# Band attention and two MLPs on one core: loads tied to places in TensorE's instruction stream, one mask kind loaded, a last block in halves

## The chip, the cores and the metric

The kernel runs on one core of one Trainium2 chip. The metric is the device time of one execution in microseconds (us), as the median of several executions. A profiled execution gives the trace from which the rows below are taken; its span runs from its first to its last instruction.

## What is computed

Attention over four batches of eight heads: 512 local rows that see keys within 32 positions and the 32 global keys, and 32 global rows that see everything. Its output passes through two MLPs of 2176 rows (4 x 544), width 512 and inner width 2048. All inputs and outputs are 32-bit.

```python
def _attn_ref(q_l, k_l, v_l, q_g, k_g, v_g):
    ...
    s_g = scale * np.matmul(q_g, k_all.transpose(0, 1, 3, 2))
    out_g = np.matmul(sm(s_g), v_all)
    ...
    mask = np.abs(pos[:, None] - pos[None, :]) <= window
    s_ll = np.where(mask, s_ll, -1000000000.0)
    s_l = np.concatenate([s_lg, s_ll], axis=-1)
    out_l = np.matmul(sm(s_l), np.concatenate([v_g, v_l], axis=2))
    ...

# first MLP:  h = x @ w_in; g = elu(h); x = g @ w_out
# second MLP: h = x @ w_in; g = 0 below -1, h above 1, (h + 1)**2 / 4 between; out = g @ w_out
```

## The kernel before

**Stages.** The first 124 us or so are attention, with a first part of the first MLP woven in; then come the two MLPs, in ten chunks of rows of weights, with TensorE nearly without a gap. Each MLP product is made of three matmuls on high and low parts (`wl x xh`, `wh x xl`, `wh x xh`).

**Units of attention.** There are 24 units, n = 0 to 23, in groups of three: the local rows of a pair of heads, the global rows of two pairs, the local rows of the second pair. There are 16 pairs, p = 0 to 15. One turn of the loop issues the scores of unit n (matmuls `s` or `sg`), the transposes of unit n-1 (`pt` or `tg`), the transposes of the output of unit n-2 (`ot`), and the product with the values of unit n-1 (`po` or `pog`). From n = 9 on, 12 matmuls of the MLP (`up`) join in each turn or two. Recording is by a wrapper, `Pinned`, so all of these have one line, L113, and stand in each engine's queue in the order of the program.

**Loads.** All of them are issued by SP (the SyncE queue, SPq), in the order of the program. For each pair these are queries (`q_sb`, 272 KB), keys (`k_sb`, 288 KB) and two halves of the values (`v_sb`, 520 KB each); six pieces of weights (`wraw`, 512 KB) come with them. After the turn of unit n, `arrive(n)` issues the queries and keys of a pair (`load_qk`), a piece of weights or some halves of values; the table `V_UNTIL` tells how far the values may run. `q_sb` and `k_sb` have two buffers each, the values six halves. A paced load (values and weights) also waits until the loads in flight together with it are at most 3200 words of each partition (`IN_FLIGHT`); queries and keys are not paced. So a load's start is set by buffers, pace and SP's order, and not by where TensorE stands.

**Start.** Ten warm-up matmuls on zeros run while queries and keys of pairs 0 and 1, the mask (three kinds, 192 KB, on ACT's queue), the identity and the values of pair 0 are loaded. VectorE copies 32 rows of each of two kinds of the mask.

**End.** `down` sums the last product in four PSUM banks (d = 0 to 3) over two rows of weights; `collect` adds each bank to `acc` on VectorE and stores 128 x 512 results from SP. After attention the order is made by a scheduler (`eng = free`).

## Time and profile before

| what | value |
|---|---|
| median of 3 runs | 863.31 us (861.24 to 863.80) |
| profiled execution | 864.74 us, its span 862.9 us |
| TensorE (PE) busy | 844.9 us, 98% of the span |
| VectorE (DVE) busy | 581.4 us, 67% |
| ScalarE (ACT) busy | 431.7 us, 50% |
| moved by DMA | 65.45 MB, of which code (q8 instruction) 48 packets, 0.79 MB |
| granted TensorE clock, mean | 0.996 of full speed |

A timeline row gives the start, the duration, the engine, the line, the operation, out<-in, the shapes and the count; in brackets stands the idle time of the engine before it and what ended it, where "issue" means that the engine waited for nothing that the profile shows. A row of a stretch gives its length, then busy time and count of each engine, the granted TensorE clock, the busy share of the DMA engines and GB/s. Every TensorE matmul here has a weight load of its own (LDWEIGHTS), a second instruction.

### The profile page before, as it was taken

The numbers are of one execution on the slowest core, as the hardware profiler recorded it, in microseconds if no ns is written. First come the engines' busy times: TensorE is split into PE (matmuls) and PEld (weight loads), VectorE is DVE, ScalarE is ACT, GpSimd is POOL, SyncE is SP. The second block draws the span as 40 slices with busy tenths as digits, with TensorE's granted clock in tenths as the row PEclk, the third lists the DMA queues.
The fourth block names the chain that finished last, engine by engine and source line by source line (L and its number), as shares of the span: only waits on it lengthen the run. The fifth ranks groups of instructions, "written<-read, shape, count | busy, mean of one in ns | idle before, by whom it ended". The sixth has DMA issues, their size and how long they took to land.

```text
span 862.9 us, 14906 instructions
## 1 busy us (share of the span) xinstructions
PE 844.9 (98%) x6138; PEld 694.0 (80%) x6138; DVE 581.4 (67%) x1130; ACT 431.7 (50%) x755; POOL 28.2 (3%) x66
## 2 busy tenths in 40 slices
PE   8799899999999999999999999999999999999998
PEld 5677778888888888888888888888888888888886
DVE  4689765879527964834399896368759754845455
ACT  5678674666335543533357564456435333433332
POOL 2122200000000000000000000000000000000000
PEclk9999999999999999999999999999999999999999
DMA  8888722222101210200022112012101200000014
GB/s 265 288 275 266 222 78 98 97 98 98 50 0 49 98 49 0 98 1 1 0 71 77 49 50 97 1 40 93 63 1 58 90 0 1 1 1 0 2 62 146
DMA packets 23124, 65.45 MB, mean 76 GB/s; under 512 B 3984, under 2 KB 4240, under 8 KB 19344
## 3 DMA queue, kind: packets, MB, share of 16 engines
q1 hardware_dynamic: 22768, 64.23, 21.8%
q8 instruction: 48, 0.79, 0.4%
q10 hardware_dynamic: 288, 0.26, 0.1%
q14 instruction: 20, 0.16, 0.1%
HBM read 60.03 MB, written 4.46 MB: 75 GB/s over the span
## 4 chain that ended last, share of the span: by engine, by line
PE 93%; DMA 3%; DVE 2%; issue 1%; ACT 1%; SPq 0%
PE dn L320 40%; PE up L247 39%; PE up L244 3%; PE dn L337 3%; PE up L113 2%; PE po L113 2%; DMA k_sb<-in_kT 1%; PE pt L113 1%; PE s L113 1%; PE sg L113 1%; PE tg L113 1%; DMA wraw<-in_w 1%; DVE top L113 1%; DMA v_sb<-in_vwin 1%; PE ot L113 1%
## 5 line engine op out<-in xcount | busy, mean ns | idle before, releaser
L320 PE MATMUL dn<-gh,wh 128*128 128x512 f32 x506 | 196.9, 389 | 0.0
L320 PE MATMUL dn<-gl,wh 128*128 128x512 f32 x506 | 196.8, 389 | 0.0
L320 PE MATMUL dn<-gh,wl 128*128 128x512 f32 x506 | 196.3, 390 | 0.0
L247 PE MATMUL up<-xh,wl 128*128 128x512 f32 x492 | 192.5, 391 | 0.0
L247 PE MATMUL up<-xl,wh 128*128 128x512 f32 x492 | 191.6, 389 | 0.0
L247 PE MATMUL up<-xh,wh 128*128 128x512 f32 x492 | 191.6, 389 | 0.0
L278 ACT ACTIVATE gh<-g 128x512 fp32r<-128x512 f32 x123 | 77.7, 632 | 118.7 <-DVE g L267 71.8
L297 DVE TENSOR_TENSOR acc<-dn,acc 128x512 f32<-128x512 f32 x128 | 84.9, 685 | 48.7 <-PE dn L320 48.4
L320 PEld LDWEIGHTS dn<-gl,wh 128*128 128x128 f32 x506 | 95.0, 188 | 19.9
L282 DVE TENSOR_TENSOR gl<-g,gh 128x512 fp32r<-128x512 f32 x123 | 84.6, 689 | 38.9 <-ACT gh L278 37.8
L320 PEld LDWEIGHTS dn<-gh,wh 128*128 128x128 f32 x506 | 95.0, 188 | 19.4
L320 PEld LDWEIGHTS dn<-gh,wl 128*128 128x128 f32 x506 | 95.0, 188 | 19.4
L247 PEld LDWEIGHTS up<-xh,wh 128*128 128x128 f32 x492 | 92.3, 188 | 19.3
L247 PEld LDWEIGHTS up<-xl,wh 128*128 128x128 f32 x492 | 92.4, 188 | 18.8
L247 PEld LDWEIGHTS up<-xh,wl 128*128 128x128 f32 x492 | 92.4, 188 | 18.7
L258 ACT ACTIVATE g<-up,half_sb 128x512 f32<-128x512 f32 (+1 forms) x69 | 47.0, 681 | 113.6 <-PE up L247 104.8
L266 DVE SCALAR_TENSOR_TENSOR g<-g 128x512 f32<-128x512 f32 (+1 forms) x69 | 46.9, 680 | 59.4 <-ACT g L258 59.3
L264 DVE SCALAR_TENSOR_TENSOR g<-up,g 128x512 f32<-128x512 f32 x64 | 43.4, 679 | 62.5 <-ACT g L255 62.5
L253 ACT ACTIVATE g<-up 128x512 f32<-128x512 f32 x64 | 37.8, 590 | 86.2 <-PE up L247 80.6
L267 DVE TENSOR_TENSOR g<-g,e 128x512 f32<-128x512 f32 (+1 forms) x69 | 46.9, 680 | 3.6
L180 ACT ACTIVATE top<-wraw 128x1024 f32<-128x1024 f32 x29 | 33.7, 1163 | 29.2 <-DMA wraw<-in_w 24.1
L255 ACT ACTIVATE g<-g,one_sb 128x512 f32<-128x512 f32 x64 | 45.8, 716 | 1.8
(112 smaller groups left out, 923.6 us busy)
## 6 DMA issues: line engine op xcount, KB each, us to landing
wraw<-in_w SPq DMA_DIRECT2D x29, 1024.0 KB, 4.8
v_sb<-in_vwin SPq DMA_DIRECT2D x32, 520.0 KB, 5.3
k_sb<-in_kT SPq DMA_DIRECT2D x16, 288.0 KB, 3.9
q_sb<-in_qT SPq DMA_DIRECT2D x16, 272.0 KB, 5.2
outT<-acc SPq DMA_DIRECT2D x16, 256.0 KB, 2.1
wraw<-in_w SPq DMA_DIRECT2D x6, 512.0 KB, 4.6
outT<-acc_rows SPq DMA_DIRECT2D x4, 64.0 KB, 2.2
mask_sb<-in_mask ACTq DMA_DIRECT2D x1, 192.0 KB, 3.4
```

The lines of the kernel that those rows point to most:

```text
L113: return lambda *args, **kw: tc.keep_in_program_order(fn(*args, **kw))
L247: eng.tensor.matmul(self.ps, w, x, start=k == 0, stop=k == 3 * KT - 1)
L253: eng.scalar.activation(self.g, self.ps, AF.Exp)
L255: eng.scalar.activation(self.g, self.g, AF.Relu, bias=one_sb, scale=-1.0)
L258: eng.scalar.activation(self.g, self.ps, AF.Relu, bias=half_sb, scale=0.5)
L264: eng.vector.scalar_tensor_tensor(g, self.ps, 0.0, g, ALU.max, ALU.subtract)
L266: eng.vector.scalar_tensor_tensor(g, g, 1.0, g, ALU.min, ALU.mult)
L267: eng.vector.tensor_tensor(g, g, self.e, ALU.add)
L278: eng.scalar.activation(self.gh, self.g, AF.Copy)
L282: eng.vector.tensor_tensor(self.gl, self.g, self.gh.bitcast(F32), ALU.subtract)
L297: eng.vector.tensor_tensor(a, ps, a, ALU.add)
L320: eng.tensor.matmul(banks[d], w[:, d * P:(d + 1) * P], g, start=f == fs[0] and k == 0, stop=f == fs[-1] and k == 2,)
```

## The change

- `Pinned` counts the instructions that it issues to TensorE: 4 for each row of the program that is a 32-bit matmul (it becomes two matmuls, each with its weight load), 2 for the others. When the count passes 186, 436.5, 687 and so on by 250.5, the matmul that passes it is called an entry into a block, and `by_blocks` issues up to three loads behind it: each waits until this matmul is done. The three are chosen by the unit that needs them first: queries and keys of a pair, a half of values, a piece of weights. There are 20 such entries with loads; all loads from pair 2's queries and pair 1's values on go there, and the pace of 3200 words no longer applies to them.
- Queries and keys have three buffers; the third one for keys lies in `acc[0]`, which is written only after attention.
- The mask: only kind 1 (64 KB) is loaded; kinds 0 and 2 are copied whole on VectorE and 32 x 32 of each is filled.
- The last output block (layer 1, last batch, d = 3) is made in two halves of 256 columns, the second of them in a bank of the up products; the first half is stored from ACT's queue, the second from SP's.

```diff
-V_UNTIL = {0: 2, 1: 4, 2: 6, 3: 7, 4: 9, 5: 11}
+AT_ONCE = 3
+
+FIRST_BLOCK, BLOCK = 186, 250.5
...
+            def issue(*args, **kw):
+                ins = tc.keep_in_program_order(fn(*args, **kw))
+                if name in ("matmul", "transpose"):
+                    self.issued += 4 if name == "matmul" and args[1].dtype == F32 else 2
+                    if self.issued > FIRST_BLOCK + self.block * BLOCK:
+                        self.block += 1
+                        at_block(ins)
+                return ins
...
-    def load(out, src, words, paced=True):
+    def load(out, src, words, paced=True, behind=None):
 
         ins = eng.sync.dma_start(out, src)
+        if behind is not None:
+            tc.add_manual_dep(ins.ins, behind.ins.name, LANDED, reason="loads by blocks")
...
+            queue = eng.scalar if at.stop < SL else eng.sync
+            queue.dma_start(outT[d, :, j * S + SG + at.start:j * S + SG + at.stop], a)
...
+            spans = [slice(0, SL)]
+            if (layer, j, fs[-1], d) == (1, B - 1, NF - 1, KT - 1):
+                spans = [slice(0, SL // 2), slice(SL // 2, SL)]
...
+                banks[d] += [up_bank() for _ in spans[1:]]
...
+        qs = [raw_p.tile([P, S], F32, name=f"q_sb{i}") for i in range(3)]
+        ks = [raw_p.tile([P, k_cols], F32, name=f"k_sb{i}") for i in range(2)]
+        ks.append(acc[0].rearrange("p d n -> p (d n)")[:, 0:k_cols])
...
-        eng.scalar.dma_start(mask_sb, mask)
+        load_qk(0)
+        eng.scalar.dma_start(mask_sb[:, 1, :], mask[:, 1, :])
+        load_qk(1)
...
-        eng.vector.tensor_copy(mask_sb[32:64, 0, :], mask_sb[32:64, 1, :])
-        eng.vector.tensor_copy(mask_sb[64:96, 2, :], mask_sb[64:96, 1, :])
+        for kind, r, c in ((0, 0, 0), (2, 96, 64)):
+            eng.vector.tensor_copy(mask_sb[:, kind, :], mask_sb[:, 1, :])
+            eng.vector.memset(mask_sb[r:r + 32, kind, c:c + 32], FILL)
...
+        def by_blocks(ins):
+
+            for _ in range(AT_ONCE):
+                found = []
+                p = now["qk"]
+                if p < len(pairs) and now["n"] >= 3 * ((p - 3) // 2) + 1 + (p - 3) % 2:
+                    found.append((3 * (p // 2) + p % 2 - 1, 0, send_qk))
+                p = len(pairs) - (len(ahead) + 1) // 2
+                if ahead and 2 * len(pairs) - len(ahead) < now["until"]:
+                    found.append((3 * (p // 2) + p % 2 + 1, 1, send_v))
+                if now["free"] and len(parts) < len(halves):
+                    found.append((3 * len(parts) + 3, 2, send_words))
+                if found:
+                    min(found, key=lambda item: item[:2])[2](ins)
...
-            if r == 1 and p + 1 < len(pairs):
-                load_qk(*pairs[p + 1])
-            elif r == 2 and p + 2 < len(pairs):
-                load_qk(*pairs[p + 2])
-            elif r == 0 and g:
-                next(next(sent, iter([0])))
-            while ahead and len(ahead) > 2 * len(pairs) - V_UNTIL.get(n, 4 * g + (4, 6, 7)[r]):
-                load_v(*ahead.pop(0))
+            now["n"] = n
+            if place == 0:
+                return
+            now["until"] = 4 * g + (6, 6, 8)[r]
+            while now["qk"] < len(pairs) and now["qk"] <= p + (r == 2):
+                send_qk()
```

On SP's queue, at the fifth piece of weights (turns n = 14 to 16), there stands before, with the semaphores that each load waits for (DMAHW: an earlier load; PE, DVE, Activation, Pool: that engine):

```order
L113 DMA q_sb<-in_qT 128x544 [waits PE_49,Pool_49]
L113 DMA k_sb<-in_kT 128x576 [waits DMAHW3_49,Pool_49]
L113 DMA v_sb<-in_vwin 128x2x520 [waits DMAHW0_49,PE_49]
L113 DMA wraw<-in_w 128x512 [waits DMAHW1_49,DVE_49,Activation_49]
L113 DMA v_sb<-in_vwin 128x2x520 [waits DMAHW6_49,DMAHW3_49,PE_49]
L113 DMA q_sb<-in_qT 128x544 [waits DMAHW7_49,PE_49,Pool_49]
L113 DMA k_sb<-in_kT 128x576 [waits PE_49]
L113 DMA v_sb<-in_vwin 128x2x520 [waits DMAHW5_49]
L113 DMA v_sb<-in_vwin 128x2x520 [waits DMAHW6_49,DMAHW2_49]
```

and now, from the entry that issues the fifth piece of weights on (`q_sb_126` and so on are the single buffers):

```order
L126 DMA wraw<-in_w 128x512 [waits DMAHW1_49,DVE_49,DMAHW4_49,PE_49,Activation_49]
L126 DMA q_sb_125<-in_qT 128x544 [waits DMAHW5_49,Pool_49]
L126 DMA k_sb_128<-in_kT 128x576 [waits DMAHW6_49,Pool_49]
L126 DMA v_sb<-in_vwin 128x2x520 [waits DMAHW7_49]
L126 DMA v_sb<-in_vwin 128x2x520 [waits DMAHW0_49,PE_49]
L126 DMA q_sb_126<-in_qT 128x544 [waits PE_49,Pool_49]
L126 DMA k_sb_129<-in_kT 128x576 [waits DMAHW2_49]
L126 DMA v_sb<-in_vwin 128x2x520 [waits DMAHW3_49]
L126 DMA v_sb<-in_vwin 128x2x520 [waits DMAHW4_49,PE_49]
```

Here four loads form a block with one wait for TensorE ahead of it, then one half of values stands alone, then four again; before, a load's wait for TensorE was that for its own buffer.

At the end of the program TensorE's last rows were

```order
L320 MATMUL dn<-gl,wh_2887 128x512
L320 MATMUL dn<-gh,wl_2888 128x512
L320 MATMUL dn<-gh,wh_2887 128x512
L320 MATMUL dn<-gl,wh_2887 128x512
L320 MATMUL dn<-gh,wl_2888 128x512
L320 MATMUL dn<-gh,wh_2887 128x512
L320 MATMUL dn<-gl,wh_2887 128x512
```

and are now

```order
L349 MATMUL dn<-gh,wh_2862 128x512
L349 MATMUL dn<-gh,wl_2863 128x256
L349 MATMUL dn<-gh,wh_2862 128x256
L349 MATMUL dn<-gl,wh_2862 128x256
L349 MATMUL dn<-gl,wh_2862 128x512
L349 MATMUL dn<-gh,wl_2863 128x256
L349 MATMUL dn<-gh,wh_2862 128x256
L349 MATMUL dn<-gl,wh_2862 128x256
```

The second half stands some 25 rows earlier (`up<-gh,wl` 128x256 and five more), so that three matmuls of 256 columns end the program, with d = 2 right ahead of them. Between the attention and this end TensorE's, VectorE's and ACT's orders are as before, but for the name of the third key buffer.

## Rows read from the trace of the kernel before

**Rows 1.** Waits of TensorE, first 130 us: us in total, times, longest

```profile
PE s L113 <- issue: 2.8, 3, 1.8
PE pog L113 <- issue: 2.7, 2, 1.4
PE po L113 <- issue: 2.4, 2, 1.9
```

**Rows 2.** Timeline of TensorE, 24 to 37 us, the wait in brackets

```profile
24.70 0.78 PE L113 MATMUL po<-v_sb,pT 128*32 128x65 f32 x40 [0.50 <-issue]
25.41 1.16 PE L113 MATMUL s<-k_sb,q_sb 64*32 64x128 f32 x64
26.50 0.87 PE L113 MATMUL tg<-eye_sb,pg 128*128 128x128 f32 x6
27.73 0.63 PE L113 MATMUL ot<-eye_sb,o_sb 128*128 128x128 f32 x4 [0.36 <-DVE o_sb L113]
28.29 0.42 PE L113 MATMUL pog<-v_sb,pgT 96*32 96x65 f32 x12
29.97 0.65 PE L113 MATMUL pog<-v_sb,pgT 96*32 96x65 f32 x14 [1.26 <-issue]
...
36.15 1.32 PE L113 MATMUL po<-v_sb,pT 128*32 128x65 f32 x51 [1.90 <-issue]
```

**Rows 3.** Timeline of TensorE, the other three long waits for "issue"

```profile
14.67 0.41 PE L113 MATMUL s<-k_sb,q_sb 64*32 64x128 f32 x4 [0.84 <-issue]
...
47.87 0.55 PE L113 MATMUL pog<-v_sb,pgT 64*32 64x65 f32 x10 [1.42 <-issue]
...
90.28 0.85 PE L113 MATMUL s<-k_sb,q_sb 64*32 64x128 f32 x38 [1.82 <-issue]
```

**Rows 4.** Stretches of one group of units each (one missing, 48.35 to 62.00)

```profile
17.49:31.39 13.90, 11.62 (x357) 9.19 (x350) 11.25 (x53) 12.21 (x35) 3.56 (x8) 1.00 0.92 301
31.39:48.35 16.96, 13.25 (x358) 10.17 (x351) 12.00 (x55) 10.49 (x29) 3.21 (x8) 0.90 0.87 279
62.00:76.69 14.69, 13.99 (x368) 11.10 (x363) 13.38 (x57) 12.34 (x33) 3.73 (x8) 1.00 0.82 262
76.69:94.90 18.21, 15.66 (x370) 12.18 (x363) 13.94 (x58) 13.00 (x35) 5.00 (x10) 0.91 0.71 228
94.90:108.97 14.07, 13.64 (x368) 10.91 (x362) 12.45 (x56) 11.78 (x31) 3.25 (x6) 1.00 0.81 257
```

**Rows 5.** Stretches of 2 us behind two of the waits

```profile
38.00:40.00 2.00, 2.00 (x15) 1.49 (x12) 1.45 (x3) 0.00 (x0) 0.00 (x0) 0.50 0.92 220
92.00:94.00 2.00, 2.00 (x31) 1.56 (x29) 0.95 (x11) 1.51 (x4) 0.00 (x0) 0.50 0.66 170
```

**Rows 6.** DMA queues, 82.31 to 90.28 us: packets, MB, share of 16 engines

```profile
q8 instruction: 1, 0.02, 1.4%
```

**Rows 7.** The same, 86.5 to 87.0 us

```profile
q8 instruction: 1, 0.02, 23.1%
```

**Rows 8.** Timeline of SP's queue, 83 to 85 us

```profile
83.84 0.95 SPq L113 DMA_DIRECT2D v_sb<-in_vwin  x2
```

**Rows 9.** Timeline of the start, VectorE and TensorE

```profile
4.63 0.47 DVE L113 COPY mask_sb<-mask_sb 32x128 f32<-32x128 f32 x2 [0.60 <-DMA mask_sb<-in_mask]
6.96 0.29 DVE L113 CUSTOM_DVE_ANT_0 sn<-s,mask_sb 128x128 f32<-128x128 f32 x1 [1.86 <-PE s L113]
...
9.07 1.14 PE L113 MATMUL sg<-k_sb,diag 128*64 128x272 f32 x10 [0.39 <-DMA k_sb<-in_kT]
...
16.36 1.21 PE L113 MATMUL pog<-v_sb,pgT 96*32 96x65 f32 x48
```

**Rows 10.** Timeline of the end

```profile
853.13 0.60 PE L347 MATMUL up<-eye_sb,acc_rows 128*128 128x128 f32 x4
...
859.25 0.69 DVE L297 TENSOR_TENSOR acc<-dn,acc 128x512 f32<-128x512 f32 x1 [0.67 <-PE dn L320]
```

**Rows 11.** Chain of work that ended last: start, us, what

```profile
853.73 5.50 PE dn L320 x24
```

More of the change, by code (lines that the diff above doesn't have):

```diff
@@ L103, in band_attention_then_two_mlps, with at_block @@
     acc = {}
+    on_block = []
+    def at_block(ins):
+        for what in on_block:
+            what(ins)
     class Pinned:
@@ L421, in load_v @@
                 src = src.rearrange("p (s a) h v -> p s (a h v)", s=2)
-                load(v_sb, src, half * 2 * VW)
+                load(v_sb, src, half * 2 * VW, paced=behind is None, behind=behind)
                 v_sb = v_sb.rearrange("p s (a h v) -> p s a h v", a=half // 2, h=2)
@@ L669, in band_attention_then_two_mlps @@
         spread_keys(*pairs[0])
-        eng.vector.tensor_copy(mask_sb[32:64, 0, :], mask_sb[32:64, 1, :])
-        eng.vector.tensor_copy(mask_sb[64:96, 2, :], mask_sb[64:96, 1, :])
+        for kind, r, c in ((0, 0, 0), (2, 96, 64)):
+            eng.vector.tensor_copy(mask_sb[:, kind, :], mask_sb[:, 1, :])
+            eng.vector.memset(mask_sb[r:r + 32, kind, c:c + 32], FILL)
         spread_queries(*pairs[1])
         def early_weights():
-            for part in parts:
+            for i in range(len(halves)):
+                while len(parts) <= i:
+                    send_words()
                 for _ in range(3):
-                    next(part, None)
+                    next(parts[i], None)
                     yield
@@ L698, in early_ups @@
                 u.low()
-        parts = [prep(g_p, wtmp_p, 0, *part, raw_tag="wraw") for part in halves]
-        sent = iter(parts)
+        parts, now = [], dict(n=0, until=4, free=True, qk=2)
         weights, ups = early_weights(), early_ups()
@@ L745, in band_attention_then_two_mlps @@
                 next(weights, None)
+            if n > 3 and n % 3 == 2:
+                now["free"] = True
             if n >= UP_AT:
```

76 lines of the change are left out of this document (44 added, 32 removed).

## The prediction

> **What bounds the kernel now.** I read the table first: TensorE is busy for 98% of the span, so only its idle time, its slow stretches and its instruction count can give anything. Its waits by cause come next: in the first 130 us the largest are waits for "issue", 2.8, 2.7 and 2.4 us, together 7.9 us in seven places [rows 1]; waits for data or for another engine are smaller there. The timeline shows what they are. From the wait that ends at 24.70 to the one that ends at 29.97 TensorE runs 40 + 64 + 6 + 4 + 12 = 126 matmuls, which are 252 instructions with their weight loads; from there to 36.15 it runs 125 [rows 2]. The page counts 48 packets of code with 0.79 MB, 16 KB each, for 2 x 6138 instructions: 256 in a packet. So TensorE waits at a border between packets, for code. Counted on from the wait that ends at 14.67 in steps of 125 matmuls, the other long waits, at 47.87 and 90.28, fall on borders too [rows 3]. Most borders pass without a wait.
>
> The DMA view tells why some don't. Between the border at about 82.31 (counted) and the one at 90.28 a single code packet moved [rows 6], and it is recorded at 86.5 [rows 7]: 4.2 us after TensorE entered the block ahead, and then it takes 23.1% of 16 engines x 0.5 us = 1.85 us. So the code of the next block is asked for about when TensorE enters a block, and comes late when the DMA engines are full of loads: some of those were issued after that border [rows 8]. [...] What it costs is read from the groups: 18.21 us against 14.69 for the undisturbed one before it, 3.52 us, of which 1.82 is the wait and 1.7 the clock; the next group is 0.62 shorter than the undisturbed one [rows 4], because VectorE had caught up. That place costs 2.9 us net. In the group of 16.96 us the mean clock is 0.90, again 1.7 us.
>
> [...]
>
> **The change part by part.**
>
> *Loads at the entries.* No byte is added: a pair is 272 + 288 + 2 x 520 = 1600 KB, 1.64 MB, and a block carries up to that. At the 321 to 327 GB/s that the two fullest stretches give at full share (279/0.87 and 301/0.92, [rows 4]) 1.64 MB take 5.0 us. Undisturbed blocks last 3.6 to 6 us (a group of 14.69 us is just under three). So where one full block of loads follows another, up to some 2 us of it is still moving when TensorE enters; where a light block comes between, nothing is.
>
> Late part, from 62 us on: the loads go in a rhythm of 1.6, 1.6 and 0.5 MB to a group. The entry that now meets the late packet, at 82.31, would carry 0.5 MB instead of three loads. I take that wait as gone, with its clock: 2.9 us. Against it, the entry behind two full blocks meets a rest of about 2 us; I charge 0.2 us for each of three groups. Sum: +2.3 us.
>
> Early part, 17.49 to 48.35: two groups take 30.86 us, with waits for code of 0.50 + 1.26 + 1.90 + 1.42 and a short one of 0.17 more, 5.25 us, and 1.7 us of clock; bare they would take 23.9 us. But here DMA is nearly full: the 301 x 13.90 + 279 x 16.96 = 8.9 MB that moved take 27.5 us at full share, while two groups need (4 x 1.6 + 2 x 0.5 MB) 7.6 MB, 23.4 us. So the gain lies between 30.86 - 27.5 = 3.4 us, if the loads must run as far ahead as now, and 6.95 us, if nothing but TensorE's work is left. Waits for code that stay would take from it: each of the five full blocks there may cost up to 1 us, so the lower bound is -1.6 us. I take +3.8, near the DMA bound, since that is the row nearest to a full queue.
>
> *What is now behind a wait.* SP's queue holds the loads in order, so everything queued waits for the entry: the first block's four loads (pair 2's queries and keys, pair 1's values) come behind the entry at about 11 us, where the values were issued a little earlier before. They need 5 us and land at 16 to 17.5; `pog` at 16.36 reads them [rows 9]. Cost 0 to 1.5 us; and with these loads still moving at the second entry, the code of the third block may be late by 0 to 2 us, partly the same time. The wait of 0.84 us at 14.67 stays as it is: the block ahead of it is short. I take -0.8 us for both. Later on, loads stand at least a turn ahead of their readers, so I charge nothing; if that cover fails, a reader waits for up to 1.7 us (one half of values at 320 GB/s). The added semaphore waits lie on SP, which computes nothing.
>
> *Third buffers.* `acc[0]` is first written after attention. No cost.
>
> *Mask.* 128 KB less ahead of pair 1's keys is 0.4 us at 320 GB/s, and TensorE waits 0.39 us for those keys at 9.07 [rows 9]: +0.3. VectorE's copies: 0.24 us each now [rows 9], as many columns in the new ones, two fills more, together under 0.8 us from 4.6 on. The first reader starts at 6.96 and waits for TensorE [rows 9], so they are hidden; without that cover they would cost 0.3.
>
> *Last block in halves.* Twelve matmuls of 256 columns stand for six of 512. The latter have a pitch of 5.50/24 = 0.229 us [rows 11], 1.37 us. A pair of weight load and matmul of 128 columns takes at most 0.60/4 = 0.15 [rows 10]; so 256 columns cost 0.115 (half of 512) to 0.19 (between the two), 1.4 to 2.3 us; I take 0.135, +0.25 us of work. Then the order: d = 2's add of 0.69 us [rows 10] still stands ahead of the last half's add on VectorE, and only some 0.4 us of matmuls lie behind d = 2; so the last add ends 0.69 + about 0.4 us behind d = 2's last matmul, where it was 0.69 + 0.69. That gives 0.3 us back, and a store half as large up to 0.3. Bounds: -0.9 to +0.6 us; I take 0.1 us lost.
>
> **Sum**: 2.3 + 3.8 - 0.8 + 0.3 - 0.1 = 5.5 us gained, a span of 857.4 and, with the 1.84 us around it, 859.2 us for the profiled execution. That one was 1.4 us above the median of the runs (863.31), so the median should come to 857.8 us.
>
> **The rivals.** *The code waits move, and DMA stays the bound.* If each entry in the full early part still meets 2 us of loads, the blocks there last as long as their loads (5 us) plus what is lost at the start, the early gain shrinks to about 0.5, and the late one to 1.5, since short blocks of 3.6 us leave no room. Then 863.3 - 0.5 - 1.5 + 0.8 - 0.2 = 862 us. For it: DMA's share of 0.92 and 0.87 [rows 4]; against it: the late part has room at 0.71 to 0.82.
>
> *Loads right behind the entry delay the very code asked for at it.* Two halves of values were issued from 83.84 on, 1.5 us behind the border at 82.31 [rows 8], and the packet came behind most of them [rows 6, 7]. The change puts 1.6 MB right there, at some twelve entries. If the packet yields to loads behind it, those blocks last 5.0 us of loads and more, some eight of them stall by about 1.5 us and two clock falls of 1.7 us come on top: 15.4 us in place of the 7.9 + 3.4 = 11.3 lost now, and the time is 867.5 us. It decides from about 6 us between entry and code on. Against it: of some twenty borders in the first 125 us most passed without a wait, though loads follow nearly every one.
>
> [...]
>
> *All of it goes.* If the code always comes before the loads and the early part runs bare: 6.95 + 2.9 + 0.3 - 0.5 = 9.6 less, 853.7 us.
>
> **How the numbers follow.** A measurement of this kernel can tell about 0.3% from no change, 2.6 us: faster is below 860.7, slower above 865.9. Forecast (854.5 to 860.7): 0.54. First rival: 0.22. Second rival: 0.16. All gone: 0.08. So faster 0.62, same 0.22, slower 0.16. The range leaves out about half of the last case and most of the second rival: 854 to 866 us.
>
> **What would show it.** Right: "issue" waits of TensorE in the first 130 us below 4 us, none at the border that stood at 90.28, a granted clock of 1.00 in 40 to 120 us, groups of 14.0 to 14.7 us from there on and of under 14 us between 17 and 48, code packets within 2 us of an entry. Wrong: waits for code of 1.5 us and more at borders behind full blocks, a clock of 0.50 behind them, or waits of `po` and `pog` for `v_sb` in place of "issue". At the end the last matmul should come 0 to 0.6 us later against the first one of the MLP, and the span end within 0.5 us of that. If the early groups stay at 30 us in all while the late part gains 3, the DMA term was the wrong one.

## The result and the profile after

The changed kernel takes 868.59 us (median of 6 runs, 868.29 to 871.65), the kernel before 863.14 in the same comparison: a ratio of 1.0073, with an interval of 1.0055 to 1.009. It is slower by 5.4 us, where 5.5 us were forecast as a gain, and it lies outside the range. The profiled executions differ by less, 868.29 against 864.74, since that of before was 1.6 us above its median and that of after 0.3 below. Of the executions reported below, one of twelve of e2 (1698.56 us) and two of six of e4 (1210.58 and 1413.14) were in a slow state; they are left out of the times and ratios, and e4's profile, which is one of them, is not read.

TensorE's waits in the first 130 us show what was exchanged for what (us in total, times, longest):

```profile
PE tg L126 <- DVE og L126: 4.4, 5, 1.1
PE pog L126 <- DMA v_sb<-in_vwin: 2.9, 2, 2.0
PE s L126 <- issue: 2.8, 4, 1.4
PE po L126 <- issue: 2.2, 4, 1.1
...
PE pog L126 <- issue: 0.5, 1, 0.5
PE po L126 <- DMA v_sb<-in_vwin: 0.6, 1, 0.6
```

The waits for code fell from 7.9 us [rows 1] to 2.8 + 2.2 + 0.5 = 5.5; waits for values rose to 2.9 + 0.6 = 3.5. The two long waits for values stand at the start, where 16.37 answers to 16.36 in [rows 9] (timeline of TensorE):

```profile
16.37 0.77 PE L126 MATMUL pog<-v_sb,pgT 96*32 96x65 f32 x24 [0.91 <-DMA v_sb<-in_vwin]
19.18 0.91 PE L126 MATMUL pog<-v_sb,pgT 64*32 64x65 f32 x22 [2.04 <-DMA v_sb<-in_vwin]
20.02 1.96 PE L126 MATMUL s<-acc,q_sb 64*32 64x128 f32 x64
21.90 1.50 PE L126 MATMUL pt<-eye_sb,sn 128*128 128x128 f32 x8
```

Unit 3 begins at 20.02, where it began at 17.49 [rows 4], and its 64 products of scores take 1.96 us and not 1.16 [rows 2]: the granted clock is 0.50 behind the wait, as the stretch of 2 us there shows (the clock is the third number from the end):

```profile
20.00:22.00 2.00, 2.00 (x69) 1.60 (x66) 0.55 (x3) 0.00 (x0) 1.59 (x4) 0.50 0.85 326
```

The groups of units, each from one start to the next (us, busy time of PE, PEld, DVE, ACT and POOL, clock, DMA share, GB/s), compare with [rows 4]:

```profile
20.02:33.06 13.04, 12.36 (x354) 9.97 (x350) 9.29 (x49) 8.29 (x22) 3.88 (x8) 0.89 0.87 292
33.06:48.95 15.89, 12.08 (x357) 9.33 (x350) 13.87 (x58) 11.87 (x34) 3.67 (x9) 1.00 0.76 255
48.95:63.14 14.19, 13.87 (x369) 11.06 (x362) 10.96 (x52) 10.61 (x28) 3.48 (x8) 1.00 0.73 244
63.14:78.55 15.41, 14.18 (x370) 11.21 (x363) 13.12 (x57) 12.35 (x33) 4.10 (x8) 1.00 0.75 248
78.55:95.08 16.53, 14.33 (x368) 11.15 (x362) 13.09 (x57) 12.33 (x33) 3.98 (x8) 1.00 0.70 233
95.08:111.48 16.40, 14.16 (x369) 11.01 (x362) 13.09 (x57) 12.34 (x33) 6.02 (x12) 1.00 0.89 292
```

The early part (two groups) takes 28.93 us and not 30.86. The group with the long wait and the slow clock shrank from 18.21 to 16.53 with a clock of 1.00, but its undisturbed neighbours of 14.69 and 14.07 became 15.41 and 16.40. The first MLP product starts at 127.13, 2.54 us later than before (124.59).

Products of the last output block, and the last adds and a store (timeline of TensorE, VectorE and ACT's queue):

```profile
856.47 0.28 PE L349 MATMUL up<-gh,wl 128*128 128x256 f32 x1
856.59 0.28 PE L349 MATMUL up<-gh,wh 128*128 128x256 f32 x1
...
861.47 1.02 DVE L320 TENSOR_TENSOR acc<-dn,acc 128x512 f32<-128x512 f32 x2 [0.35 <-PE dn L349]
...
862.52 0.35 ACTq L334 DMA_DIRECT2D outT<-acc  x1
```

The rows show TensorE's early 256-column products, which went into a bank of the up products (`up`), then VectorE's last two adds and ACT's store. VectorE is done at 862.49, 2.55 us later than before, so the lateness of the attention went through unchanged. From there to the end of the span it is 4.0 us, where it was 3.0.

### The profile page after: what moved, and what is told of

It reads as the page before. It is cut to its first block, busy times and chain, and to the rows that moved or that the text cites. A ratio compares the mean times of both kernels' runs of the same rounds, so it can differ in the third digit from the quotient of the medians.

```text
span 866.5 us, 14909 instructions
## 1 busy us (share of the span) xinstructions
PE 844.5 (97%) x6144; PEld 693.5 (80%) x6144; DVE 581.2 (67%) x1133; ACT 431.2 (50%) x755; POOL 29.0 (3%) x66
## 4 chain that ended last, share of the span: by engine, by line
PE 93%; DVE 3%; DMA 2%; ACT 1%; issue 1%; SPq 0%; DVEq 0%
PE dn L349 40%; PE up L270 39%; PE up L267 3%; PE dn L366 3%; DMA v_sb<-in_vwin 2%; PE up L126 2%; PE po L126 2%; PE pt L126 1%; PE s L126 1%; PE sg L126 1%; DVE top L126 1%; PE tg L126 1%; PE idle L126 1%; PE dn L126 0%; DVE xl L126 0%
## 5 line engine op out<-in xcount | busy, mean ns | idle before, releaser
L349 PE MATMUL dn<-gh,wh 128*128 128x512 f32 (+1 forms) x506 | 196.7, 389 | 0.0
L349 PE MATMUL dn<-gh,wl 128*128 128x512 f32 (+1 forms) x506 | 195.9, 389 | 0.0
L276 ACT ACTIVATE g<-up 128x512 f32<-128x512 f32 x64 | 37.9, 592 | 86.5 <-PE up L270 81.2
L282 ACT ACTIVATE e<-up,nhalf_sb 128x512 f32<-128x512 f32 (+1 forms) x69 | 46.6, 676 | 0.3 <-DVE g L290 0.3
```

The lines of the kernel that those rows point to most:

```text
L276: eng.scalar.activation(self.g, self.ps, AF.Exp)
L282: eng.scalar.activation(self.e, self.ps, AF.Relu, bias=nhalf_sb, scale=0.5)
L349: eng.tensor.matmul(bank[:, at], w[:, d * P:(d + 1) * P], g[:, at], start=f == fs[0] and k == 0, stop=f == fs[-1] and k == 2,)
```

## The experiments

One table holds what the profiles and times of all kernels say: TensorE's waits in the attention for code ("issue"), for loads (`v_sb`, `k_sb`) and for VectorE (`og`, `o_sb`), the start of the first MLP product, the time of the profiled execution, the median, and the ratio to the kernel before, measured beside it. One profile is one execution, and executions of one kernel differ by up to 12.7 us (858.12 to 870.8 us for the kernel before, in the comparison with e1), so sums of waits go with the profiled time and not with the median.

| kernel | code | loads | VectorE | MLP at | profiled | median | ratio, interval |
|---|---|---|---|---|---|---|---|
| before | 7.9 | 0.6 | 3.1 | 124.59 | 864.74 | 863.14 | |
| after | 5.5 | 3.5 | 5.3 | 127.13 | 868.29 | 868.59 | 1.0073, 1.0055 to 1.009 |
| e1 | 7.4 | 0.8 | 2.7 | 122.16 | 862.43 | 861.93 | 0.9989, 0.996 to 1.0017 |
| e6 | 6.3 | 0.9 | 3.9 | 123.85 | 864.06 | 862.37 | 0.9994, 0.9974 to 1.0015 |
| e2 | 7.5 | 0 | 3.5 | 122.72 | 863.57 | 864.53 | 1.0028, 1.0006 to 1.0049 |
| e3 | 3.6 | 3.9 | 5.5 | 126.99 | 867.64 | 867.75 | 1.0059, 1.0036 to 1.0082 |
| e5 | 5.8 | 0 | 7.8 | 128.37 | 869.02 | 864.65 | 1.0028, 1.0011 to 1.0046 |
| e8 | 6.5 | 3.9 | 5.0 | 133.62 | 873.78 | 874.54 | 1.0136, 1.0109 to 1.0164 |
| e9 | 3.3 | 8.6 | 2.6 | 132.73 | 873.39 | 871.35 | 1.01, 1.0065 to 1.0135 |
| e10 | 3.4 | 12.7 | 1.2 | 139.08 | 879.61 | 879.61 | 1.0197, 1.0172 to 1.0221 |
| e7 | 2.7 | 0 | 4.8 | 115.57 | 855.89 | 855.89 | 0.9919, 0.9892 to 0.9947 |
| e13 | 7.2 | 0 | 3.9 | 124.95 | 865.27 | 864.94 | 1.0002, 0.9982 to 1.0022 |
| e14 | 6.6 | 0 | 2.9 | 123.28 | 863.62 | 867.05 | 1.0039, 1.0004 to 1.0074 |
| e15 | 1.1 | 0 | 5.4 | 116.59 | 856.78 | 857.19 | 0.9942, 0.9914 to 0.9969 |
| e11 | 4.4 | 0 | 6.8 | 122.65 | 863.30 | 866.16 | 1.0031, 1.0012 to 1.005 |
| e12 | 6.9 | 2.7 | 5.8 | 128.74 | 869.42 | 864.78 | 1.0017, 0.9995 to 1.0039 |
| e16 | 5.1 | 2.1 | 5.1 | 125.44 | 866.18 | 864.36 | 1.0021, 1.0002 to 1.004 |
| e17 | 5.8 | 2.1 | 5.0 | 123.79 | 864.47 | 863.86 | 1.0015, 0.9997 to 1.0033 |
| e18 | 4.1 | 2.8 | 5.4 | 126.81 | 867.52 | 867.81 | 1.0049, 1.0026 to 1.0072 |

### Which part of the change lost the time

**The end alone (e1):** the kernel before with the last output block in halves.

```diff
+            if (layer, j, fs[-1], d) == (1, B - 1, NF - 1, KT - 1):
+                spans = [slice(0, SL // 2), slice(SL // 2, SL)]
```

> The kernel before with the two halves of the last output block alone. In the trace after, the last add of VectorE ends 2.55 us later than before, as all of the attention does, but the span ends 3.6 us later. Theory (the end has a cost of its own): 4.0 us instead of 3.0 us from the last add to the end of the span, about 864.1 us against 863.1, a ratio of 1.001. Rival (the end is neutral and the last 1 us is that execution's): the ratio is 1.000 and the stretch from the last add to the end stays at 3.0 us.

861.93 us, 0.9989: no difference. The 4.0 us behind the last add in the profile of after are 3.1 here with the same end, so most of the 1 us more is not the end's. Some of it comes back, though: the nine other profiles of the changed kernel with all its loads have 3.4 to 3.7. Why is open. In e1 TensorE runs the attention in the order of before, and yet it reaches the MLP at 122.16 and not at 124.59: from one execution to another it is different borders that wait.

**The mask alone (e6):** the kernel before with one kind loaded and two made on VectorE.

```diff
-        eng.scalar.dma_start(mask_sb, mask)
+        eng.scalar.dma_start(mask_sb[:, 1, :], mask[:, 1, :])
...
+        for kind, r, c in ((0, 0, 0), (2, 96, 64)):
+            eng.vector.tensor_copy(mask_sb[:, kind, :], mask_sb[:, 1, :])
+            eng.vector.memset(mask_sb[r:r + 32, kind, c:c + 32], FILL)
```

> Kernel before with the mask part alone: one kind loaded, two made on VectorE. Theory: pair 1's keys come 0.4 us earlier, TensorE's wait of 0.39 us at 9 us goes and nothing else moves: 862.0 to 863.0 us, within noise of the kernel before. Rival (the copies of whole kinds on VectorE, or the shifted places of the borders against the loads, cost what the start lost): 864.5 to 866 us, unit 3's scores later than 17.5 us.

862.37 us, 0.9994: as the theory had it. Its unit 3 starts at 16.52, and TensorE does not wait for the keys there. But it does not wait for them in e1 either, which has the mask of before, so the profiles do not tell the mask's 0.4 us from the spread between executions.

**Pair 1's values at the start (e2), the weights one turn later (e3), both (e5):** the changed kernel with one line each.

```diff
         load_v(*pairs[0])
+        load_v(*pairs[1])
...
-        ahead = [(*pair, (e,)) for pair in pairs[1:] for e in range(2)]
+        ahead = [(*pair, (e,)) for pair in pairs[2:] for e in range(2)]
...
-            if n > 3 and n % 3 == 2:
+            if n > 3 and n % 3 == 0:
```

> The kernel after, but pair 1's values are issued at the start right behind pair 0's, behind no entry. Theory (the start lost 2.5 us because these values wait for the first entry): the waits of 0.91 and 2.04 us of the first pog for v_sb and the half clock behind them go, unit 3's scores start at about 17.5 us instead of 20.0, and the time falls by 2 to 3 us from 868.6 to about 866. Rival (the start only hid later code waits, the early part is bound by DMA): unit 3 starts earlier but unit 9's scores start at 48.5 to 49 us as before, and the time stays within 0.7 us of 868.6.

> The kernel after, but each piece of weights from the second on may be asked for one unit later, when VectorE is done reading the piece before. Theory (the piece of weights waits on SP's queue for VectorE's last reader, 15.1 us in five waits, and the loads behind it start 2 to 4 us into their block, so that the next entry meets them): SP's waits for DVE top fall below 4 us, the waits for issue at the entries behind full blocks go down, groups from unit 9 on take 14.7 us instead of 15.4 to 16.5, and the time falls by 2 to 4 us to about 865.5. Rival (loads right behind an entry delay the code whatever their order): the waits for issue stay at 5 us in all and the time within 0.7 us of 868.6.

> Changed kernel with both corrections at once: pair 1's values issued at the start as before, and a piece of weights only offered to the entries one turn later, when VectorE is done with its single buffer. Theory (the code that is asked for at an entry comes behind the loads still moving at it; beside that the change lost 3 to 4 us at the start and about 1 us to the weights' wait on SP): the two add, so 863.5 to 865 us, within 0.3% of the kernel before, with waits for code that stay at 4 to 7 us. Rival (the loads issued right behind an entry delay that entry's code): nothing of that changes, waits for code stay at 5.5 us or more and the time at 866 to 868 us.

e2 takes 864.53 us, 4.1 less than the changed kernel. Its start (timeline of TensorE) has no wait for values, and unit 3 begins at 17.32:

```profile
14.54 0.41 PE L126 MATMUL s<-k_sb,q_sb 64*32 64x128 f32 x4 [0.69 <-issue]
...
16.23 1.16 PE L126 MATMUL pog<-v_sb,pgT 96*32 96x65 f32 x48
17.32 1.16 PE L126 MATMUL s<-acc,q_sb 64*32 64x128 f32 x64
```

The gain was not eaten by later waits: unit 9 begins at 45.11, where it began at 48.95. So some 4 of the 5.4 us lie in the values of pair 1, which the change put behind an entry (1.5 to 6 by the two intervals). e3 takes 867.75, 0.8 less, which its interval does not tell from nothing and which misses the 2 to 4 us of the theory, though SP's waits for VectorE's `top`, 15.1 us in the changed kernel against 7.0 before, fell to 1.3. e5 has both at 864.65. What is left, 1 to 2.4 us, has no loads late; in the profile, which is of its longest execution, there are 5.8 us of waits for code, 7.8 for VectorE and one of 1.7 us for POOL's work on the third key buffer.

### Which loads delay a block's code

**Entries in the middle of blocks (e4), two loads in flight (e8):**

```diff
-FIRST_BLOCK, BLOCK = 186, 250.5
+FIRST_BLOCK, BLOCK = 311, 250.5
```

```diff
-IN_FLIGHT = 3200
+IN_FLIGHT = 2200
```

> The kernel after with the first entry at 311 instead of 186, so that all loads are issued in the middle between two places where code is asked for. Theory (where loads stand against the borders matters, since code asked for while loads move comes behind them): the next border comes 2 to 3 us behind 1.6 MB of loads that need 5 us, code waits rise to 10 us and more with falls of the clock, and pair 1's values come still later: 873 to 880 us. Rival (code is delayed by the load on DMA as such, not by the place): the waits for issue stay near 5 us, and only the later start of the first loads costs, 870 us.

> Kernel before with 2200 instead of 3200 words of paced loads in flight: two loads at a time instead of three. Theory (code comes behind the loads that still move when it is asked for): less stands ahead of the code at an entry, waits for code fall from 7 to 8 us to 4 to 6 us, but values may come late in the early part, where the DMA engines are nearly full: 861 to 864 us. Rival (the loads issued behind an entry decide): the waits for code stay at 7 us or more and any later values come on top: 863 to 866 us.

e4 is 878.6 us, 1.0192 (1.0149 to 1.0236), where a later start alone was put at 870. So the place against the borders seems to matter, and right behind them to be better than between them; how much of the 10 us more than the changed kernel takes is code and how much values that start later still is not shown. e8, an edit of the kernel before, missed the theory's range by 10.5 us: the waits for code went from 7.9 to 6.5 us, but SP waited 66.0 us for earlier loads (10.7 before) and loads came late by 3.9 us. The pace of 3200 words is no brake that could be drawn tighter.

**No loads (e7):** later pairs read the tiles of the earlier ones.

```diff
             for sb, dram in both if p else both[::-1]:
+                if p > 2:
+                    break
...
+                p = pairs.index((b, hp))
+                if p > 1:
+                    landed.setdefault((b, hp), []).append(landed[pairs[p % 2]][e])
+                    continue
```

> Changed kernel without the loads of queries and keys from pair 3 on and of values from pair 2 on: later pairs read the tiles of the earlier ones (so the output is not the attention's). TensorE's instructions stay; of the loads behind entries only pair 2's queries and keys and the six pieces of weights are left. Theory: with nothing moving at an entry its code comes within 1.3 us and no wait of TensorE for code is left behind unit 6 (under 0.5 us each); the attention's groups take 12 to 12.5 us early and 13.6 to 14.2 us late, the first MLP product starts 10 to 14 us earlier than in the changed kernel, so 855 to 858 us. Rival (fetching code is slow by itself at these borders, whatever the loads do): waits for code of 4 us and more stay, 861 to 865 us.

855.89 us, inside the range of the theory. Of TensorE's waits the two largest that remain are (first 140 us):

```profile
PE tg L126 <- DVE og L126: 4.0, 6, 0.8
PE s L126 <- issue: 2.7, 2, 2.5
```

The 2.5 us stand at 14.95, where the first loads still move; behind unit 3 no border waits. So the loads make all the other waits for code, and some 7 us (4.6 to 9.3 by the interval) are the most that any arrangement of them can give. The groups settle at 14.6 us and not lower (14.14, 14.64, 14.65, 14.63), and the wait that is left in them is for VectorE's `og`.

That it is the code packet that TensorE waits for shows in the 19 profiles of the table: each of the 86 waits for "issue" of over 0.25 us at a border ends 1.2 to 1.6 us behind the end of the code packet recorded in the block before (worked out from packets and matmuls, borders 2 to 21). At the 288 borders without a wait of over 0.15 us that packet had ended 1.2 us ahead or more. The middle packet of the 48 in the trace of before takes 1.0 us, that of after 1.05. So, as an estimate from these times, a block that is shorter than the packet's delay behind its entry and some 2.4 us ended in a wait here.

**A bundle of its own at the entries (e13), three quarters (e14) and a quarter (e15) of a block behind them:** e7 with two halves of values into tiles that nobody reads, one half in e15.

```diff
+        def probe(ins):
+            ...
+            for sb in probes[len(parts) > now["parts"]:]:
+                load(sb, src, half * 2 * VW, paced=False, behind=ins)
...
+            if 3 <= pinned.tensor.block <= 20:
+                probe(ins)
```

> The kernel without loads (later pairs read the earlier pairs' tiles) with a bundle of its own at each entry from the third to the twentieth: two halves of values into tiles that nobody reads (1.06 MB, 3.2 us; one of them stands back for a piece of weights where there is one). The bundle starts right behind the entry and is done before the next, so at an entry nothing is moving. Theory (code comes behind the loads that move when it is asked for): the packets come 0 to 1.5 us behind the entries, as without loads, waits for code stay below 1 us behind the third block, the time within 1.5 us of the run without loads (855.9). Rival (loads issued right behind an entry delay that entry's code): packets come 3.5 to 5 us behind the entries, waits for code sum to 5 us or more, 860 us or more. Both in part: packets in two groups, most within 1.5 us and some at 3.5 to 5.

> The same with each bundle three quarters of a block behind an entry (188.5 of 250.5 instructions), so that 2 to 3 us of it still move at the next entry and nothing is issued in the 2.5 us behind that one. Theory: packets come 2.5 to 4 us behind the entries, waits for code sum to 4 to 9 us behind the third block, the time 4 to 12 us above the run with the bundles at the entries. Rival: packets within 1.5 us, waits below 1 us, the time 4 us or more below that run.

> The same with one half of values (0.53 MB, 1.6 us) a quarter of a block (about 1.2 us) behind each entry; the load is done before the next entry. Theory: nothing moves at an entry, packets within 1.5 us, no waits for code, time as without loads (855 to 857 us). If code is asked for later than at the counted entry: some packets at 2.5 to 4 us, waits of 0 to 2 us in all.

e13 costs 7 to 9 us against e7 (864.94; 7.2 by the ratios, 9.0 by the medians), far over what the theory allowed, and it shows the rival at work. Two entries of one execution, by the DMA queues (packets, MB, share of 16 engines) and the loads issued (KB, us to landing). First the stretch from the entry at 57.08 to 58.5:

```profile
q1 hardware_dynamic: 6, 0.02, 12.8%
q8 instruction: 1, 0.02, 4.2%
probe<-in_vwin SPq DMA_DIRECT2D x2, 520.0 KB, 4.9
```

Then those from the entry at 26.03 to 29.5, and from there to 30.0:

```profile
q1 hardware_dynamic: 164, 0.62, 59.6%
probe<-in_vwin SPq DMA_DIRECT2D x2, 520.0 KB, 5.0
...
q1 hardware_dynamic: 48, 0.19, 95.1%
q8 instruction: 1, 0.02, 12.1%
```

At 57.08 the two loads went out 0.43 and 0.80 us behind the entry, and the code packet came 1.15 us behind it, ahead of nearly all their data. At 26.03 they went out 0.27 and 0.81 us behind it, the 3.5 us up to 29.5 hold 0.62 MB of data and no code, and the packet starts at 29.75, behind them. TensorE then stood, and the clock fell, to 0.50 from 34 to 36 us:

```profile
29.68 0.42 PE L126 MATMUL pog<-v_sb,pgT 96*32 96x65 f32 x13
32.17 1.33 PE L126 MATMUL pog<-v_sb,pgT 96*32 96x65 f32 x35 [2.08 <-issue]
33.44 1.96 PE L126 MATMUL s<-k_sb,q_sb 64*32 64x128 f32 x64
```

Late in the attention the program's count of instructions is off in these kernels. The waits of e13 and e14 stand 126 matmuls apart (at matmul 595, 1980 and 2107, and at 595, 721, 1351, 1729, 2107, 2358 and 2485), those of the kernels with all loads 125.25. So the loads of e13's entries 15 to 17 were issued ahead of the border by up to 1 us, and its late packets there are cases of loads that still move; those of its third and fourth entry are not.

e15 takes 857.19 us, with 1.1 us of waits for code, all at the start. It carries half the bytes, so it is no clean twin; but from its fourth border on, counted in steps of 126, the packets come 0.4 to 1.4 us behind the border, but for 2.3 at the fifteenth. That one is as late in e7 (2.3), where next to nothing moves, so its code comes late by itself. e14, with 2.0 to 5.4 us of loads still moving at each border, has 6.6 us of waits in its profile and takes 867.05. That is 2.1 us above e13 and inside the noise, where the theory wanted 4 to 12.

Over 19 traces, entries 3 to 20, the packet's delay goes with what has still to land of the loads issued before TensorE got to the entry (worked out from packets, landings and matmuls counted from the 93rd in steps of 125.25, of 126 in the four kernels without loads; where TensorE waits at a border, the entry is the end of the wait; 342 entries):

| last landing behind the entry | under 1 us | 1 to 2 | 2 to 3 | 3 to 4 | 4 to 5 | over 5 |
|---|---|---|---|---|---|---|
| entries | 80 | 53 | 67 | 74 | 35 | 33 |
| mean delay of the packet, us | 1.31 | 1.26 | 1.90 | 2.66 | 2.88 | 3.39 |
| packets over 3 us late | 7 | 5 | 9 | 16 | 21 | 23 |

In the first column little still moves, and there the loads issued behind the entry can be seen by themselves: of its 25 entries with a load issued within 0.4 us behind them 7 have a packet over 3 us late (the third and fourth of e13, and one each in e2, e3, e5, e9 and e11), of the other 55 none. Both go with late packets in these traces: loads that still move, with a mean delay of 1.31 us in the first column and 3.39 in the last, and, at these 7 of 25 entries, loads issued in the entry's first 0.4 us. This border of 0.4 us was read off the same entries and not tested on others. Whether the code is asked for a little later there, or asked for in time and kept waiting, no trace here shows.

### Bundles cut to the blocks

**Two loads at most entries (e9), the same a quarter of a block later (e10):** on e5.

```diff
-            for _ in range(AT_ONCE):
+            for _ in range(AT_ONCE if pinned.tensor.block % 3 == 0 else 2):
```

> Changed kernel with pair 1's values at the start, the weights one turn later, and bundles cut to the blocks: three loads only at every third entry, two at the others, so that a bundle (3.2 to 3.4 us of loads, 5.0 at the third) ends before TensorE enters the next block (3.5 to 6 us without waits, from the run without loads). Each bundle still starts right behind its entry. Theory (the code comes behind the loads that still move when it is asked for): little moves at the entries, waits for code fall from 5.8 us to 1 to 3 us, no clock of 0.50 behind unit 9, the first MLP product starts at 118 to 121 us and the time is 858 to 861 us. Rival (loads issued right behind an entry delay that entry's code): 1.0 to 1.6 MB still follow nearly every entry, so waits for code stay at 5 us or more and the time at 864 to 866 us.

> The same with the loads a quarter of a block (62 of 250.5 instructions, about 1.2 us) behind the entries. Theory (loads still moving at an entry are what delays its code): every bundle reaches 1.2 us further into the next block, the waits for code grow by 1 to 3 us against the run with sized bundles, and the time is 1 to 3 us longer than there. Rival (loads issued right behind the entry delay its code): the code now has 1.2 us ahead of them, the waits for code fall below those of the run with sized bundles, and the time is 2 us or more shorter than there.

e9 did to the code what the theory said and missed the time by 10 us. Its waits (first 130 us):

```profile
PE pog L126 <- DMA v_sb<-in_vwin: 8.6, 7, 1.8
PE s L126 <- issue: 3.3, 3, 1.7
```

Of the 3.3 us of waits for code 1.7 are the start's and 1.4 one border's, the sixteenth. But two, two and three loads are just the seven that three blocks need, so the lateness from the start is never made good: seven times the global rows wait for half a pair's values, and the mean clock from 51.2 us on is 0.91. In e10 no border behind the third waits over 0.3 us for code, as the rival had it, and values are late by 12.7 us with `po`'s and `pog`'s waits. In both runs an entry as the only gate starved the readers (8.6 and 12.7 us of waits for loads) once the waits for code were down to 3.3 and 3.4 us.

**Three loads early, cut bundles late (e11), half of pair 1's values at the start (e12):**

```diff
-            for _ in range(AT_ONCE):
+            for _ in range(2 if block > 9 and block % 3 == 1 else AT_ONCE):
```

```diff
-        load_v(*pairs[1])
+        load_v(*pairs[1], (0,))
...
+            for _ in range(2 if block == 1 or block > 9 and block % 3 == 1 else AT_ONCE):
```

> Changed kernel with pair 1's values at the start, the weights one turn later, three loads at each entry up to the ninth (as in the run with both corrections), and from the tenth on two loads at the entry into the short block (3.5 us) and three at the other two: each bundle of 3.2 to 5.0 us fits its block, and the values stand a half further ahead than in the run with sized bundles. Theory (code comes behind the loads that still move at its entry; the sized run lost its gain only to values half a turn late): behind the ninth entry waits for code stay below 1.5 us and waits for values below 2 us, the stretch from the ninth to the twenty-second entry takes 66 to 69 us instead of 72.2 (run with both corrections) and 69.7 (changed kernel), and the time is 859.5 to 863 us. Rival (loads right behind an entry delay its code): the late waits for code stay at 3 us, the time at 864 to 866 us.

> The same, but only the first half of pair 1's values is loaded unbound at the start, the second behind the first entry with pair 2's queries and keys alone; everything else of the early part moves down by up to one load. Theory: less moves at the second entry than with ten loads unbound (there TensorE waited 1.7 to 2.5 us for the third block's code), so the wait for code at the third block falls below 1 us, the second half lands in time, unit 3's scores start at 17 us or earlier and the time is 1 us or so below that of the run with late sized bundles, 858.5 to 862.5 us. Rival (the start's loss is the values' lateness alone, whatever is loaded beside them): the second half of the values is waited for by 1 us or more, and the time is 1 to 2 us longer than there.

In e11's profiled execution no border behind the ninth entry waits, no load is late, and the time is 863.30, with 6.8 us of waits for VectorE in place of those for code. But its median is 866.16, 3 us above the theory's range: over the other executions the gain does not hold. e12, at 864.78, is not to be told from the kernel before; its profiled execution was its longest, with waits for code of 2.2 us at the sixth border and 3.2 at the twentieth: the packet came 6.7 us behind the nineteenth entry, where 3.7 us were still to land and two halves of values were issued 0.4 and 0.8 us behind it.

**Loads 0.6 us (e16) and 1.2 us (e17) behind the late entries, 0.6 us behind all (e18):** on e12, with the loads of each entry kept but for some pieces of weights.

```diff
-                    if self.issued > FIRST_BLOCK + self.block * BLOCK:
+                    entry = FIRST_BLOCK + self.block * BLOCK
+                    if self.issued > entry + 31 * (self.block > 8):
```

> The kernel of e12 (half of pair 1's values at the start, bundles cut to the blocks behind the ninth) with the loads from the ninth entry on issued 31 instructions, about 0.6 us, behind their entries; the loads of each entry stay the same but for two pieces of weights. Theory in its new form (a block's code is asked for some 0.3 to 1.2 us behind the counted entry and comes behind all that was asked for before it, so loads right behind an entry win that race now and then): fewer late packets than with the loads at the entries, waits for code behind the ninth entry below 2 us (4.2 in the profile of e12), 860 to 863.5 us. Without that race: as e12, 864.8 us, within 1 us.

> The same with 62 instructions, about 1.2 us. New theory: the code now has a lead at every late entry but where 5.0 us of loads follow an entry into a block of 5.3 us; waits for code behind the ninth entry below 1 us, but values may be waited for by 1 to 3 us in all; 859.5 to 864 us. Without the race: loads reach 1.2 us further into the next blocks, 866 to 868 us.

> As the first of these, with the 0.6 us at every entry but the first. New theory: in the early part the DMA engines are nearly full, so 0.6 us later loads at each entry come back as values' waits or as loads that still move at the next entry: no gain there, 861 to 865 us, not below the first by more than 1 us. Without the race: 865 to 867 us.

864.36, 863.86 and 867.81 us. The first two are 0.4 and 0.9 us below e12, in the direction of the new theory and inside the noise. A lead of 1.2 us in the count does not settle it: in e17 the packet came 5.3 us behind the seventeenth border, where 3.0 us were still to land and the next loads went out 0.8 us and more behind it. The delay throughout (e18) comes out 3 us above e12, at the edge of the noise and above both ranges. No kernel here that computes the attention is shown to be faster than the one before: e1 and e6 lie within its noise, and e7 and e15 leave the loads out.

## Why the prediction was wrong, step by step

**What bounds the kernel** was read rightly. TensorE waits at borders of 125 matmuls for code, and all of it but the start's comes from the loads (e7: 855.89 us). In e7 and e15 no border behind the start waits; in the kernel before the waits for code came to 7.9 us [rows 1]. Behind two of them, of 1.90 us [rows 2] and 1.82 us [rows 3], the granted clock was 0.50 from 36.64 to 40.05 us and from 91.25 to 94.66 [rows 5]; the loss of 1.7 us at each is an estimate, half of 3.41 us. That the code of the next block is asked for about when TensorE enters a block was inferred, and no trace shows the asking; where next to nothing moved (e7, e15), most packets started 0.4 to 1.4 us behind the border.

**The first block's values** were the largest single error. The term was 0.8 us lost, with a bound of 1.5; the profile shows waits of 0.91 and 2.04 us and a clock of 0.50 behind the second, and e2 gives back some 4 us. The four loads were priced as 5.0 us of bytes from the entry at about 11 on, landing at 16 to 17.5. The last of them was issued only at 13 us, shared the engines with pair 3's queries and keys issued at 13.9 and 14.4, and landed at 19.1 (timeline of SP's queue):

```profile
10.95 1.48 SPq L126 DMA_DIRECT2D acc<-in_kT  x1
12.48 0.96 SPq L126 DMA_DIRECT2D v_sb<-in_vwin  x2
13.93 0.34 SPq L126 DMA_DIRECT2D q_sb<-in_qT  x1
14.37 0.36 SPq L126 DMA_DIRECT2D k_sb<-in_kT  x1
```

The landing at 19.1 was not the entry at about 11 plus 5.0 us of bytes. And the clock, which I had charged for waits for code, fell to 0.50 behind a wait of 2.04 us for values too.

**The late part** was forecast as 2.3 us gained. From unit 12 to the first MLP product it took 62.59 us before and 63.99 after: 1.4 lost. The clock part of the late border's 2.9 us was won: it stayed at 1.00. But in place of one wait of 1.82 us [rows 3] there are four, 3.1 us in all. The longest two:

```profile
91.86 0.85 PE L126 MATMUL s<-acc,q_sb 64*32 64x128 f32 x38 [0.86 <-issue]
...
108.48 0.64 PE L126 MATMUL s<-k_sb,q_sb 64*32 64x128 f32 x24 [1.39 <-issue]
```

The waits for VectorE's `og` went from 2.5 to 3.3 us besides.

The failed step is the 5.0 us that a full bundle was taken to need from its entry, and with it the rest of up to 2 us at the next entry and the 0.2 us charged for each entry behind two full blocks. In the changed kernel there are eleven blocks in which 1592 or 1600 KB were issued: the last load went out 1.7 to 3.5 us behind the entry and landed 7.3 to 10.3 us behind it, where undisturbed blocks last 3.6 to 6 us. So at the entries 11, 12, 14, 15, 17 and 18 loads had still 3.0 to 5.2 us to land, and the packets came 3.1 to 4.8 us behind the entry. The fifteenth shows the chain. TensorE enters the block at 84.69, the packet falls into the view from 89.0 to 89.6 (it starts at 89.47 and ends at 90.44), and TensorE goes on past the next border 1.4 us later, at 91.86:

```profile
84.69 0.22 PE L126 MATMUL po<-v_sb,pT 128*32 128x65 f32 x1 [0.49 <-issue]
...
q8 instruction: 1, 0.02, 10.1%
```

The mean rest over entries 3 to 20 is 2.8 us after and 3.4 before, and packets over 3 us late are 7 after and 5 before. The entries were not cleared; the same bytes met them in another order. The delay that the prediction read for this block before, 4.2 us from 82.31 to 86.5 [rows 7], took the start of the view for that of the packet: it starts at 86.98, 4.9 us behind its entry.

**The early part** gained 1.9 us where 3.8 were forecast (30.86 to 28.93), inside its bounds: its waits for code fell from 5.25 us to 1.7, but one slow stretch stayed (0.89 over 13.04 us), and the waits for VectorE grew from 0.6 to 2.0 us. **The weights** on SP's queue, which I let stand free ("loads stand at least a turn ahead"), held the queue 1.3 to 3.8 us behind their entries; the price was 0.8 us at most (e3). **VectorE** was not in the sum: as TensorE waits less for code, `og` and `o_sb` are late next, 5.3 us after against 3.1, and 4.8 even with no loads (e7).

**The mask** (0.3 us) is not shown: unit 2's scores start 0.7 us earlier after (11.87 against 12.56), but at 11.93 in e1 too, which has the mask of before; e6 is within the noise, as 0.3 us must be. **The last block** (0.1 us lost) was right: the 256-column matmuls have a pitch of 0.12 us, where 0.135 was taken, and e1 is 0.9989. **Third buffers** were charged nothing, and in the changed kernel TensorE did not wait for them; in e5 it did, once, by 1.7 us.

**The rivals.** The second, loads right behind the entry, priced at 867.5 us, came nearest in time, by luck in the main. By it the packet yields to loads behind the entry at eight or so blocks; seven entries in all the traces show that by themselves, while at all seven late packets of the changed kernel loads from before the entry had still 3.0 us or more to land. And most of the 5.4 us was neither, but the values at the start. The argument against it, that most borders passed though loads follow nearly every one, holds.

**How the numbers followed.** The range took the start's bound of 1.5 us and the late part's 0.2 us each as firm. By the two profiles the start lost 2.5 us, the early part gained 1.9, the group from unit 9 to unit 12, which was not in the sum, lost 0.5 and the late part 1.4: together 2.5 us lost up to the MLP, where 5.6 were to be gained. The end of the span added 1.0. The other 1.9 us of the 5.4 lie between the profiled executions and the medians.

## What to carry to other kernels

Where TensorE waits for code at block borders, first take all loads away in a copy of the kernel: that one run shows how much of it any order of the loads can give back (here some 7 us of 863), and what is late next (here VectorE). A load is worth moving behind an event only if what it lands at, read from the last landing and not from bytes by bandwidth, is still ahead of its reader; here the first blocks had no such slack (pair 1's values landed at 19.1 us, and their reader had stood for 2.04 us). Here, with the DMA engines 70 to 90% busy, moving bundles about moved the waits about, and executions of one kernel differed by more than the gain.

## What was unexpected of the hardware

- A code packet's own time was 0.9 to 1.5 us in most places, and TensorE went on 1.2 to 1.6 us behind its end (86 waits). With next to nothing moving (e7, e15) a packet started 0.4 to 1.4 us behind the border, but for the fifteenth in both (2.3 us) and the third and sixth in e7 (2.1 and 1.8). What delays the fifteenth was not found.
- The length of a wait did not tell whether the clock fell. Behind 2.08 us in e13 (at 32.17, clock of 34 to 36 us) and 2.04 us for values in the changed kernel (20 to 22 us) it was 0.50; behind 2.54 us in e7 (at 14.95) and 2.04 us at the sixth border of e2 (36 to 38 us) it stayed at 1.00. Stretches of 2 us there and behind, e7 (the clock is the third number from the end):

```profile
15.00:17.00 2.00, 1.97 (x38) 1.53 (x37) 1.64 (x15) 1.01 (x3) 1.10 (x2) 1.00 0.38 143
17.00:19.00 2.00, 2.00 (x104) 1.52 (x94) 1.36 (x7) 2.00 (x8) 1.70 (x7) 1.00 0.00 0
```

  and in e13 behind its wait of 1.99 us at 15.04, the same border:

```profile
15.00:17.00 2.00, 1.96 (x12) 1.76 (x12) 1.55 (x15) 0.60 (x2) 0.93 (x2) 0.64 0.51 195
17.00:19.00 2.00, 2.00 (x48) 1.32 (x47) 0.92 (x5) 1.59 (x5) 1.70 (x7) 0.51 0.02 4
```

- The same instructions in the same order waited at different borders from one execution to the next: the attention is the same in e1 and before, and the MLP started at 122.16 and 124.59 us.
